# Two tiles of 128x64 in place of four of 128x32 for the projection products of two attention blocks on one core

## The chip, the core and the metric

The kernel runs on one core of a Trainium2 chip. The metric is the device time of one execution in microseconds (us). Beside the times of several runs there is one profiled execution, of which every instruction's start and length is known; its own time and its span (first to last instruction) are given separately.

## What is computed

Two attention blocks, A and B, work on separate inputs of 2048 tokens with 1024 features (32 heads of 32), in bfloat16. Their outputs are put side by side.

```python
# A: plain attention over all 2048 tokens
qkv = x @ wqkv;  p = softmax(q @ k.T * Dh ** -0.5);  a = (p @ v) @ wo
# B: four segments of 512 tokens, one after the other
p = softmax(qs @ ks.T * scale + mask)            # causal within the segment
a_dot = p @ vs
num, den = phi(qs) @ M, phi(qs) @ z + 1e-6       # memory of the segments before
o = g * num / den + (1 - g) * a_dot              # g = sigmoid(beta), per head
M, z = M + phi(ks).T @ vs, z + sum(phi(ks))      # phi(t) = t + 1 if t > 0 else exp(t)
b = o @ wo
```

## The kernel before, in words

**Names of the engines.** PE multiplies matrices, ACT computes exponentials, DVE and POOL do elementwise work, SP issues the transfers. PE holds one operand (the weights, loaded by an instruction of its own) and streams the other past it; the result goes to the memory called `ps`, which has eight banks of 512 float32 columns on 128 rows. The array of 128x128 can be used as several tiles: a tile of 128x32 takes 128 rows of the contraction and gives 32 rows of output, and four of them stand side by side. `tile_position` says where a tile stands.

**The heads in groups.** Four heads make a group of 128 feature columns; A has eight groups, B eight for each segment. For one group the work goes through these stages:

- *Projections.* Queries and keys of a group come out transposed, 128 features by tokens: the weights are a 128x128 block of `W_A` or `W_B`, the streamed operand 512 tokens of `xT_A` or `xT_B`, and eight such steps add up over the 1024 input features (`job_KA`, `job_KB`, through `proj_job`, line 1492). Values come out with tokens on the rows (`job_VA`, line 1697, 256 columns wide; `job_VB`, line 1738). B's memory has two products (`job_mem`, line 1788) and the update of M with its 128-wide steps (`job_M`, line 1810). The output projections run through `job_out` (line 1845), `job_part`, `job_whole` and `job_last` (lines 1921 to 1956). All of these hand a 128x128 block of weights to the helper `mm4` (line 773), which issues it as four tiles of 128x32, each with a matmul of its own on the same streamed operand. In the profile all their instructions stand at line 778. DVE then copies each finished bank out (`evict`, line 1489).
- *Scores* (line 1140). Keys are the weights, queries are streamed; the contraction is one head's 32 features, so four heads run in four tiles of 32x128, 32 rows each.
- *Exponential* (line 1228). ACT takes two banks, 1024 columns, at a time. A part of the exponentials is computed by a polynomial on DVE and POOL (lines 1177, 1186, 1187).
- *Value products and sums* (`round`, line 1286). For each of four heads a tile of 128x32 multiplies 32 value columns with the exponentials (line 1320), and a second set with a matrix of ones gives the row sums (line 1327). They add up in bank 7; afterwards the result is divided by the sums on DVE and POOL.

Two other kinds of product also use tiles of 128x32 and do not go through `mm4`: the guard products of lines 1512 and 1565, which find bounds for the exponential. The values of A's first group (`job_V0`, line 1715) use the whole array, 128x128, at line 1723.

**What sets the order.** Every operation is handed to a planner with an engine, a length in us, a key and the data that it reads and writes (`pe`, line 770, for PE). `schedule` (line 381) goes through a modelled time and puts each engine's operations in a fixed order: scores are urgent and come when ACT will need them, and projections and value products fill PE's time in between. It knows the modes "col" (all 128x32 products and all of the `mm4` ones), "row" (scores) and "full" (line 1723), and adds 0.10 us in the model where the mode changes. Then `rearrange` (line 565) moves single operations by the long written-out list `MOVES`. `emit` turns the dependences into semaphore waits. At run time each engine goes through its own list in order; nothing is reordered between engines but by those waits. Scores have three slots of two banks each (`SLOT_BANKS`), projections one bank (6), so the next projection waits until DVE has emptied it. `halves` (line 1475) cuts a projection step of 512 columns into two of 256, so that the second half of a bank can wait for its copy by itself; where both halves end up next to each other in PE's list, one instruction of 512 columns takes their place.

The helper before:

```python
def mm4(self, e, out, w, x, start, stop):
    for t in range(4):
        r = slice(32 * t, 32 * t + 32)
        ins = e.matmul(out[r], w[:, r], x, start=start, stop=stop, tile_position=(0, 32 * t), skip_group_check=True)
    return ins
```

Of the kernel before, what the change touches and what calls it, by code (L numbers as in the profile page):

```python
# [11 lines left out]
P = 128  # L12
# [6 lines left out]
L = 512  # L19
# [726 lines left out]
class _Kernel:  # L746
# [23 lines left out]
    def pe(self, fn, dur, key, reads=(), writes=(), mode="col"):  # L770
        return self.pg.op("PE", fn, dur, key, reads, writes, mode=mode)

    def mm4(self, e, out, w, x, start, stop):

        ins = None
        for t in range(4):
            r = slice(32 * t, 32 * t + 32)
            ins = e.matmul(out[r], w[:, r], x, start=start, stop=stop, tile_position=(0, 32 * t), skip_group_check=True)  # L778
        return ins

    def dma(self, fn, sem, key, reads=(), writes=(), issue=0.4, lat=3.0, eng="SP", gate=False):
# [710 lines left out]
    def proj_job(self, key, wt, rw, xt, rx, ncol, dst, rdst, behind=None):  # L1492
        b = self.xbank()
        out = self.ps[:, 512 * b:512 * b + ncol]

        self.halves(b, lambda e, i, c, st, en: self.mm4(e, out[:, c], wt[:, i, :], xt(i)[:, c], st, en), 8,
                    lambda i: [rw] + rx(i), dst, out, rdst, key + 1.0, key, behind)

    def square(self, kind, src, rsrc, key):
# [99 lines left out]
    def plan_prologue(self):  # L1599
# [6 lines left out]
        dummy, rd = self.sq["B"][0], self.r_sq["B"][0]  # L1606

        def warm(key, n, dur, behind=None):
            for _ in range(n):
                o = self.pe(lambda e: self.mm4(e, self.ps[:, 512 * 5:512 * 6], dummy[:, 0:P], dummy[:, :], True, True), dur, key,  # L1610
                            [rd], [self.bank[5]])
                if behind:
                    o.order.add(behind)
# [16 lines left out]
        def quarter(key, c, banks):  # L1630
            for i, kq in [(i, kq) for lo in (0, 4) for kq in range(2) for i in range(lo, lo + 4)]:
                    b = banks[kq]
                    o = self.pe(lambda e, i=i, kq=kq, b=b: self.mm4(
                        e, self.ps[:, 512 * b:512 * b + 512], self.WA[0][:, kq, i, :],
                        self.xT[:, i, 512 * c:512 * c + 512], i == 0, i == 7), 0.2165, key,
                        [self.r_WA[0][kq], self.r_xT[i][c]], [self.bank[b]])
                    if c:
                        o.order.add(self.first_ge)
            self.last_quarter = o
            if not c:  # L1640
                warm(key, WARM[1], 0.2165, o)
            sq = []
            for kq in range(2):
                dst = self.KQA[:, 0, kq, 512 * c:512 * c + 512]
                src = self.ps[:, 512 * banks[kq]:512 * banks[kq] + 512]
                bk, rd = self.bank[banks[kq]], self.r_KQA[0][kq][c]
                if c or not kq:
                    self.dve(lambda e, dst=dst, src=src: e.tensor_copy(dst, src), 512, key, [bk], [rd])
                else:
                    self.act(lambda e, dst=dst, src=src: e.activation(dst, src, ACT.Copy), 512, key, [bk], [rd])  # L1650
            for kq in range(2):
                sq += 2 * [self.square("A", self.KQA[:, 0, kq, 512 * c:512 * c + 512], self.r_KQA[0][kq][c], key)]
            if c == 0:
                for x in self.r_KQA[0]:
                    mark(x, "KQ", 0)
                self.colrun = self.guard_cols(key, sq, bank=3)
                self.guard_end(key, [self.colrun], 2, [BIAS_PART[0]], bank=4, urgent=True)
                self.first_ge = self.last_ge
            else:
                self.guard_more(key, sq, 0, *BIAS_PART[:2])  # L1660
                self.early_gc = self.last_gc
# [35 lines left out]
    def job_VA(self, g2, tp, key, bank=None, behind=None):  # L1697
        vs = g2 % 2
        holds(self.r_WAv, "W", g2)
        holds([r[tp // 2] for r in self.r_xT], "x")  # L1700
        mark(self.r_VA[vs][tp], "V", g2)
        b = self.xbank() if bank is None else bank
        dst, src = self.VA[vs][:, 2 * tp:2 * tp + 2, :].rearrange("p a b -> p (a b)"), self.ps[:, 512 * b:512 * b + 512]

        for k in range(2):
            t, c = 2 * tp + k, slice(QC * k, QC * k + QC)
            for i in range(8):
                o = self.pe(lambda e, i=i, t=t, c=c, k=k: self.mm4(e, src[:, c], self.xT[:, i, P * t:P * t + P], self.WAv[:, i, :],
                                                                   i == 0 and k == 0, i == 7), 0.11, key,
                            self.r_WAv + [self.r_xT[i][tp // 2]], [self.at(b)])  # L1710
# [27 lines left out]
    def job_VB(self, s, tt, hh, key):  # L1738
        holds([self.r_WBv], "W", s, hh)
        holds([self.r_xTB], "x", s)  # L1740
        mark([self.r_VB[tt][hh]], "V", s)
        b = self.xbank()
        src, dst = self.ps[:, 512 * b:512 * b + 512], self.VB[:, tt, 512 * hh:512 * hh + 512]

        self.halves(b, lambda e, i, c, st, en: self.mm4(e, src[:, c], self.xTB[:, i, P * tt:P * tt + P], self.WBv[:, i, c], st, en), 8,
                    lambda i: [self.r_WBv, self.r_xTB], dst, src, [self.r_VB[tt][hh]], key + 1.0, key)

    def job_KB(self, s, j, kq, key):
# [39 lines left out]
    def job_mem(self, s, j, key):  # L1788
        holds(self.r_PKQ[j % 2], "P", s, j)
        holds([self.r_Mb[j], self.r_zf[j]], "M", s - 1)  # L1790
        holds(self.r_OTB[j], "out", s - 1)
        mark(self.r_OTB[j], "mem", s)
        PQ = self.PKQ[j % 2][:, 1, :]
        rp = self.r_PKQ[j % 2][1]
        z = j % 2
        self.dve(lambda e: e.tensor_scalar(self.Zb[:, z, :], self.maskbd[:, :], self.zf[:, j:j + 1], None, ALU.mult), P / 2,
                 key - 1.0, [self.r_zf[j], self.r_c], [self.r_Zb[z]])
        b = self.xbank()
        self.pe(lambda e: self.mm4(e, self.ps[:, 512 * b:512 * b + L], self.Zb[:, z, :], PQ, True, True), 0.2165, key,
                [self.r_Zb[z], rp], [self.xr])  # L1800
        T2, r2 = self.recip_rows(self.ps[:, 512 * b:512 * b + L], [self.xr], L, key + 0.3, add=1e-6)
        b2 = self.xbank()
        self.pe(lambda e: self.mm4(e, self.ps[:, 512 * b2:512 * b2 + L], self.Mb[:, j, :], PQ, True, True), 0.2165,
                key, [self.r_Mb[j], rp], [self.xr])
        self.dve(lambda e: e.scalar_tensor_tensor(out=self.OTB[:, j, :], in0=self.ps[:, 512 * b2:512 * b2 + L],
                                                  scalar=self.gc[:, 0, j:j + 1], in1=T2[:, 0:L], op0=ALU.mult,
                                                  op1=ALU.mult), L, key + 0.5, [self.xr] + r2 + [self.r_g],
                 list(self.r_OTB[j]))

    def job_M(self, s, j, key):  # L1810
# [11 lines left out]
        b = self.xbank()  # L1822

        def mm(e, k):
            ins = None
            for t in range(4):
                ins = self.mm4(e, self.ps[:, 512 * b + P * k:512 * b + P * k + P], self.PKt[:, k, P * t:P * t + P],
                               self.VB[:, t, P * (j + k):P * (j + k) + P], t == 0 and k == 0, t == 3)
            return ins
        for k in range(2):  # L1830
# [14 lines left out]
    def job_out(self, kind, row, half, key, lhs, rl, wo, rwo, bank=None, ev="DVE", wcol=None):  # L1845
# [5 lines left out]
        assert ev == "DVE"  # L1851
        wcol = 512 * half if wcol is None else wcol

        self.halves(b, lambda e, j, c, st, en: self.mm4(e, src[:, c], lhs(j), wo(j)[:, wcol:wcol + 512][:, c], st, en), 8,
                    lambda j: rwo(j) + rl(j), ob[:, :], src, [ro], key + 1.0, key)
        col = (0 if kind == "A" else D) + 512 * half
        dst = self.out[0][P * row:P * row + P, col:col + 512]
# [63 lines left out]
    def job_part(self, row, hf, k, key):  # L1921

        b = self.xbank()
        c = row // 2
        src = self.ps[:, 512 * b:512 * b + 512]

        def reads(j):
            holds(self.wo_A(j)[1], "Wo")
            if j < 6:
# [1 line left out]
            return self.wo_A(j)[1] + ([self.r_xT[j][row // 4]] if j < 6 else [self.r_OTx[0][c]])  # L1931
        holds(self.r_KQB[k], "KQ", 3, k)
        mark(self.r_KQB[k], "part", k)
        self.halves(b, lambda e, j, cs, st, en: self.mm4(e, src[:, cs], self.xT[:, j, P * row:P * row + P],
                                                         self.wo_A(j)[0][:, 512 * hf:512 * hf + 512][:, cs], st, en), 7,
                    reads, self.part(k), src, self.r_KQB[k], key + 1.0, key)

# [3 lines left out]
    def job_whole(self, row, hf, k, b, key):  # L1941
# [4 lines left out]
        for j in range(7):  # L1946
            wo, rw = self.wo_A(j)
            holds(rw, "Wo")
            if j < 6:
                holds([self.r_xT[j][row // 4]], "OT")  # L1950
            rx = [self.r_xT[j][row // 4]] if j < 6 else [self.r_OTx[0][row // 2]]
            self.pe(lambda e, j=j, wo=wo: self.mm4(e, src, self.xT[:, j, P * row:P * row + P], wo[:, 512 * hf:512 * hf + 512],
                                                   j == 0, False), 0.2165, key, rw + rx, [self.at(b)])

    def job_last(self, row, hf, k, b, key, ev="DVE"):
# [4 lines left out]
        self.pe(lambda e: self.mm4(e, src, self.xT[:, 7, P * row:P * row + P], wo[:, 512 * hf:512 * hf + 512], ev == "DVE", True),  # L1960
                0.2165, key, rw + [self.r_OTx[1][row // 2]], [self.at(b)])
        ob = self.KQB[:, k, 0, :]
        if ev == "ACT":
# [170 lines left out]
```

## Time and profile before

| | |
|---|---|
| time, median of 3 runs | 1086.79 us (1085.61 to 1088.75) |
| time of the profiled execution | 1085.08 us |
| its span | 1083.3 us |
| matmuls and weight loads on PE | 24,916 each |
| instructions in all | 54,725 |
| mean granted PE clock | 1.00 of full speed |

How to read the rows of the profile. A group's row has the line, the engine, the operation and what it writes and reads; for a matmul or a weight load (LDWEIGHTS, on "PEld") the tile's rows and columns follow (128\*32 is 128 rows by 32 columns), then the shape of the streamed operand, and the count. Behind the bar stand the time in which at least one of them ran, the mean ns of one, and the engine's idle time just before them with what ended it. In a row of the timeline the first number is the start in us from the beginning of the span, the second how long the merged stretch lasted, its modelled end included. Matmuls overlap, so the time that PE needs for one is read from start to start. A row of the table by stage has the stretch, its length, then busy us and count for PE, PEld, DVE, ACT and POOL, the granted PE clock, the mean share of the transfer engines and GB/s. The chain is followed back from the last instruction: at each step to what released it, or to the one before it on its engine.

### The profile page before, as it was taken

The page shows a single profiled execution, that of the slowest core. Times are in us where ns is not written, and L with a number is a line of the kernel's source. Part 1 is how long each engine was busy: PE and PEld are TensorE (multiplying, and loading weights), DVE is VectorE, ACT ScalarE, POOL GpSimd, SP SyncE. Part 2 cuts the span into 40 slices and gives each one's busy share as a digit, 9 for nine tenths or more (in the row PEclk, how much of TensorE's full clock was granted, in tenths as well). Part 3 has the DMA queues.
Part 4 walks back from the last instruction along what each step waited for, and adds up shares of the span by engine and source line. Part 5 has one row for each costly group of instructions (what it writes and reads, how often), then busy time and mean ns, then how long its engine had stood idle before and what let it go on. Part 6 is the DMA issues. An engine that isn't in the chain of part 4 may idle for free.

```text
span 1083.3 us, 54725 instructions
## 1 busy us (share of the span) xinstructions
PE 1029.5 (95%) x24916; PEld 551.4 (51%) x24916; DVE 747.0 (69%) x1639; ACT 1006.5 (93%) x1192; POOL 674.5 (62%) x853
## 2 busy tenths in 40 slices
PE   8999999999999899989999998999999989999997
PEld 4456545556554454456554444465544445445554
DVE  3456667775756988887757898878647788774433
ACT  5999989998999989998999998999999789999997
POOL 1005656676657686977758687777747568866521
PEclk9999999999999999999999999999999999999999
DMA  9032350006212430032321322122121830022101
GB/s 209 8 83 52 80 131 20 11 20 142 53 36 78 114 83 18 6 95 65 87 79 40 76 51 49 26 76 76 33 87 41 247 91 4 32 71 71 42 23 51
DMA packets 171096, 71.96 MB, mean 66 GB/s; under 512 B 134768, under 2 KB 169072, under 8 KB 170864
## 3 DMA queue, kind: packets, MB, share of 16 engines
q1 hardware_dynamic: 168496, 67.66, 25.2%
q8 instruction: 196, 3.21, 1.2%
q10 hardware_dynamic: 2368, 0.79, 0.3%
q14 instruction: 36, 0.29, 0.1%
HBM read 45.23 MB, written 11.67 MB: 53 GB/s over the span
## 4 chain that ended last, share of the span: by engine, by line
PE 51%; ACT 37%; DVE 6%; DMA 2%; issue 2%; POOL 1%; SPq 0%; ACTq 0%; DVEq 0%; POOLq 0%
ACT P L1228 36%; PE ps L778 26%; PE ps L1140 10%; PE ps L1320 7%; PE ps L1327 7%; DMA Wo_B<-in_B_wo_dram 1%; PE ps L1723 1%; DVE Y L1177 1%; DVE T L1345 1%; DVE KQ_B L1490 1%; DMA W_A<-in_A_wqkv_dram 1%; DMA W_B<-in_B_wk_dram 0%; POOL Z L1186 0%; ACT P L1207 0%; PE ps L1512 0%
## 5 line engine op out<-in xcount | busy, mean ns | idle before, releaser
L1228 ACT ACTIVATE P<-ps 128x1024 bf16<-128x1024 f32 (+1 forms) x1176 | 994.8, 988 | 56.8 <-PE ps L1140 24.0
L1186 POOL TENSOR_TENSOR Z<-Y 128x512 f32<-128x512 f32 x280 | 299.5, 1074 | 237.1 <-DVE Y L1177 210.7
L1327 PE MATMUL ps<-P,onesb 128*32 128x256 bf16 (+1 forms) x4400 | 300.2, 270 | 0.1
L1320 PE MATMUL ps<-P,V_A 128*32 128x256 bf16 x3632 | 258.3, 274 | 1.2 <-DVE V_A L1733 0.6
L1177 DVE TENSOR_SCALAR Y<-ps 128x512 f32<-128x512 f32 x232 | 158.9, 685 | 98.9 <-PE ps L1140 94.7
L1140 PE MATMUL ps<-KQ_A 32*128 32x256 bf16 x4096 | 203.7, 272 | 16.1 <-ACT P L1228 8.9
L1187 POOL TENSOR_SCALAR Pc<-Z 128x512 bf16<-128x512 f32 x232 | 149.5, 649 | 23.5 <-PE ps L1320 8.2
L1140 PEld LDWEIGHTS ps<-KQ_A 32*128 32x128 bf16 x4096 | 62.7, 92 | 170.1 <-ACT P L1228 115.8
L1327 PEld LDWEIGHTS ps<-P,onesb 128*32 128x32 bf16 x4400 | 129.1, 96 | 30.9 <-issue 14.6
L778 PE MATMUL ps<-xT_B,W_B 128*32 128x512 bf16 (+1 forms) x2188 | 139.1, 367 | 5.5 <-issue 1.4
L778 PE MATMUL ps<-xT_A,W_A 128*32 128x512 bf16 (+1 forms) x2160 | 137.7, 369 | 1.8 <-DMA W_A<-in_A_wqkv_dram 1.2
L1320 PEld LDWEIGHTS ps<-P,V_A 128*32 128x32 bf16 x3632 | 108.2, 96 | 38.2 <-issue 15.5
L1253 POOL TENSOR_SCALAR_AFFINE_SELECT P<-P 128x768 bf16<-128x768 bf16 (+1 forms) x96 | 75.6, 800 | 71.1 <-ACT P L1228 70.7
L1327 PE MATMUL ps<-Pc,onesb 128*32 128x256 bf16 x464 | 118.6, 273 | 0.0
L1320 PE MATMUL ps<-Pc,V_A 128*32 128x256 bf16 x464 | 118.5, 274 | 0.1
L778 PEld LDWEIGHTS ps<-xT_B,W_B 128*32 128x32 bf16 x2188 | 53.3, 96 | 49.7 <-issue 22.3
L1345 DVE STREAM_TRANSPOSE T<-ps 128x256 f32<-128x256 f32 (+1 forms) x148 | 70.9, 481 | 10.4 <-PE ps L1327 7.5
L778 PEld LDWEIGHTS ps<-xT_A,W_A 128*32 128x32 bf16 x2160 | 51.2, 96 | 45.8 <-issue 12.0
L778 PE MATMUL ps<-Wo_B,OT_B 128*32 128x512 bf16 (+1 forms) x1064 | 71.4, 373 | 2.3 <-DMA Wo_B<-in_B_wo_dram 2.1
L1490 DVE CAST outsb<-ps 128x512 bf16<-128x512 f32 x56 | 38.6, 690 | 50.4 <-PE ps L1320 27.3
L1360 DVE STREAM_TRANSPOSE T<-rc 128x256 f32<-128x256 f32 (+1 forms) x152 | 71.8, 476 | 1.9
L778 PE MATMUL ps<-Wv_B,xT_B 128*32 128x512 bf16 (+1 forms) x1092 | 70.3, 368 | 1.1 <-DVE cols L1519 0.8
(103 smaller groups left out, 1200.1 us busy)
## 6 DMA issues: line engine op xcount, KB each, us to landing
Wv_B<-in_B_wv_dram SPq DMA_DIRECT2D x32, 256.0 KB, 3.8
W_B<-in_B_wk_dram SPq DMA_DIRECT2D x32, 256.0 KB, 3.3
W_B<-in_B_wq_dram SPq DMA_DIRECT2D x32, 256.0 KB, 4.0
Wo_B<-in_B_wo_dram SPq DMA_DIRECT2D x32, 256.0 KB, 3.7
out_dram<-outsb SPq DMA_DIRECT2D x56, 128.0 KB, 1.9
W_A<-in_A_wqkv_dram SPq DMA_DIRECT2D x14, 256.0 KB, 4.5
ot_a_scratch<-OTst SPq DMA_DIRECT2D x50, 64.0 KB, 1.7
xT_A<-ot_a_scratch SPq DMA_DIRECT2D x6, 512.0 KB, 6.7
```

The costliest lines, as they stand in the source:

```text
L778: ins = e.matmul(out[r], w[:, r], x, start=start, stop=stop, tile_position=(0, 32 * t), skip_group_check=True)
L1140: ins = e.matmul(out, kap, qap, start=st, stop=True, tile_position=(32 * h, 0), skip_group_check=True)
L1177: o = self.dve(lambda e: e.tensor_scalar(Y[:, :], src, SCALE, MID, ALU.mult, ALU.add), 512, key - 9.0, [self.bank[bank]], [rY], fixed=0.15)
L1186: self.pool(lambda e: e.tensor_tensor(Z[:, :], Y[:, :], Y[:, :], ALU.mult), 512, key, [rY], [rZ], rate=0.58)
L1187: return self.pool(lambda e: e.tensor_scalar(dst, Z[:, :], C2, REST, ALU.mult, ALU.add), 512, key, [rZ], [rP], rate=TS_RATE)
L1228: a = self.act(guarded if early else lambda e: e.activation(dst, src, ACT.Exp, scale=SCALE), cols, key, rd, wr, fixed=EXP_FIXED)
L1253: self.pool(lambda e: e.affine_select(v, v, pattern=pat, compare_op=ALU.is_ge, fill=0.0, base=0, channel_multiplier=-1), 2 * nd * P, key + ...
L1320: ins = e.matmul(self.ps[32 * h:32 * h + 32, 512 * obk + q0:512 * obk + q0 + nq], v, p, start=first, stop=last, tile_position=(0, 32 * h), ...
L1327: ins = e.matmul(self.ps[32 * h:32 * h + 32, lcol + q0:lcol + q0 + nq], self.onesb[:, 0:32], p, start=False, stop=last, tile_position=(0, ...
L1345: self.dve(lambda e: e.transpose(T2[:, 0:n], src), n, nk, rsrc, [r2], fixed=0.17)
L1360: self.dve(lambda e: e.transpose(T2[:, 0:n].rearrange("p (b r) -> p b r", r=32), bc), n, key, [rr], [r2], fixed=0.17)
L1490: self.dve(lambda e: e.tensor_copy(dst, src), 512, key, [self.at(b)], rdst, fixed=0.155)
```

## The change

The helper now issues two tiles of 64 columns, and has a new name:

```diff
-    def mm4(self, e, out, w, x, start, stop):
+    def mm2(self, e, out, w, x, start, stop):
 
         ins = None
-        for t in range(4):
-            r = slice(32 * t, 32 * t + 32)
-            ins = e.matmul(out[r], w[:, r], x, start=start, stop=stop, tile_position=(0, 32 * t), skip_group_check=True)
+        for t in range(2):
+            r = slice(64 * t, 64 * t + 64)
+            ins = e.matmul(out[r], w[:, r], x, start=start, stop=stop, tile_position=(0, 64 * t), skip_group_check=True)
         return ins
```

Every call of `mm4` becomes one of `mm2`, with the same arguments: in `proj_job`, `warm` and `quarter` (the prologue), `job_VA`, `job_VB`, `job_mem`, `job_M`, `job_out`, `job_part`, `job_whole` and `job_last`. One of them:

```diff
-        self.halves(b, lambda e, i, c, st, en: self.mm4(e, out[:, c], wt[:, i, :], xt(i)[:, c], st, en), 8,
+        self.halves(b, lambda e, i, c, st, en: self.mm2(e, out[:, c], wt[:, i, :], xt(i)[:, c], st, en), 8,
                     lambda i: [rw] + rx(i), dst, out, rdst, key + 1.0, key, behind)
```

The lengths and modes that these calls hand to the planner are untouched, and so are scores, value products, sums and the guard products.

More of the change, by code (lines that the diff above doesn't have):

```diff
@@ L1609, in warm @@
             for _ in range(n):
-                o = self.pe(lambda e: self.mm4(e, self.ps[:, 512 * 5:512 * 6], dummy[:, 0:P], dummy[:, :], True, True), dur, key,
+                o = self.pe(lambda e: self.mm2(e, self.ps[:, 512 * 5:512 * 6], dummy[:, 0:P], dummy[:, :], True, True), dur, key,
                             [rd], [self.bank[5]])
@@ L1632, in quarter @@
                     b = banks[kq]
-                    o = self.pe(lambda e, i=i, kq=kq, b=b: self.mm4(
+                    o = self.pe(lambda e, i=i, kq=kq, b=b: self.mm2(
                         e, self.ps[:, 512 * b:512 * b + 512], self.WA[0][:, kq, i, :],
@@ L1707, in job_VA @@
             for i in range(8):
-                o = self.pe(lambda e, i=i, t=t, c=c, k=k: self.mm4(e, src[:, c], self.xT[:, i, P * t:P * t + P], self.WAv[:, i, :],
+                o = self.pe(lambda e, i=i, t=t, c=c, k=k: self.mm2(e, src[:, c], self.xT[:, i, P * t:P * t + P], self.WAv[:, i, :],
                                                                    i == 0 and k == 0, i == 7), 0.11, key,
@@ L1743, in job_VB @@
         src, dst = self.ps[:, 512 * b:512 * b + 512], self.VB[:, tt, 512 * hh:512 * hh + 512]
-        self.halves(b, lambda e, i, c, st, en: self.mm4(e, src[:, c], self.xTB[:, i, P * tt:P * tt + P], self.WBv[:, i, c], st, en), 8,
+        self.halves(b, lambda e, i, c, st, en: self.mm2(e, src[:, c], self.xTB[:, i, P * tt:P * tt + P], self.WBv[:, i, c], st, en), 8,
                     lambda i: [self.r_WBv, self.r_xTB], dst, src, [self.r_VB[tt][hh]], key + 1.0, key)
@@ L1798, in job_mem @@
         b = self.xbank()
-        self.pe(lambda e: self.mm4(e, self.ps[:, 512 * b:512 * b + L], self.Zb[:, z, :], PQ, True, True), 0.2165, key,
+        self.pe(lambda e: self.mm2(e, self.ps[:, 512 * b:512 * b + L], self.Zb[:, z, :], PQ, True, True), 0.2165, key,
                 [self.r_Zb[z], rp], [self.xr])
@@ L1802, in job_mem @@
         b2 = self.xbank()
-        self.pe(lambda e: self.mm4(e, self.ps[:, 512 * b2:512 * b2 + L], self.Mb[:, j, :], PQ, True, True), 0.2165,
+        self.pe(lambda e: self.mm2(e, self.ps[:, 512 * b2:512 * b2 + L], self.Mb[:, j, :], PQ, True, True), 0.2165,
                 key, [self.r_Mb[j], rp], [self.xr])
@@ L1826, in mm @@
             for t in range(4):
-                ins = self.mm4(e, self.ps[:, 512 * b + P * k:512 * b + P * k + P], self.PKt[:, k, P * t:P * t + P],
+                ins = self.mm2(e, self.ps[:, 512 * b + P * k:512 * b + P * k + P], self.PKt[:, k, P * t:P * t + P],
                                self.VB[:, t, P * (j + k):P * (j + k) + P], t == 0 and k == 0, t == 3)
@@ L1852, in job_out @@
         wcol = 512 * half if wcol is None else wcol
-        self.halves(b, lambda e, j, c, st, en: self.mm4(e, src[:, c], lhs(j), wo(j)[:, wcol:wcol + 512][:, c], st, en), 8,
+        self.halves(b, lambda e, j, c, st, en: self.mm2(e, src[:, c], lhs(j), wo(j)[:, wcol:wcol + 512][:, c], st, en), 8,
                     lambda j: rwo(j) + rl(j), ob[:, :], src, [ro], key + 1.0, key)
@@ L1933, in job_part @@
         mark(self.r_KQB[k], "part", k)
-        self.halves(b, lambda e, j, cs, st, en: self.mm4(e, src[:, cs], self.xT[:, j, P * row:P * row + P],
+        self.halves(b, lambda e, j, cs, st, en: self.mm2(e, src[:, cs], self.xT[:, j, P * row:P * row + P],
                                                          self.wo_A(j)[0][:, 512 * hf:512 * hf + 512][:, cs], st, en), 7,
@@ L1951, in job_whole @@
             rx = [self.r_xT[j][row // 4]] if j < 6 else [self.r_OTx[0][row // 2]]
-            self.pe(lambda e, j=j, wo=wo: self.mm4(e, src, self.xT[:, j, P * row:P * row + P], wo[:, 512 * hf:512 * hf + 512],
+            self.pe(lambda e, j=j, wo=wo: self.mm2(e, src, self.xT[:, j, P * row:P * row + P], wo[:, 512 * hf:512 * hf + 512],
                                                    j == 0, False), 0.2165, key, rw + rx, [self.at(b)])
@@ L1959, in job_last @@
         src = self.ps[:, 512 * b:512 * b + 512]
-        self.pe(lambda e: self.mm4(e, src, self.xT[:, 7, P * row:P * row + P], wo[:, 512 * hf:512 * hf + 512], ev == "DVE", True),
+        self.pe(lambda e: self.mm2(e, src, self.xT[:, 7, P * row:P * row + P], wo[:, 512 * hf:512 * hf + 512], ev == "DVE", True),
                 0.2165, key, rw + [self.r_OTx[1][row // 2]], [self.at(b)])
```

## The prediction

> **What bounds the kernel now.** I read the page's busy shares first, then the shares of the chain that ended last.
>
> ```profile
> span 1083.3 us, 54725 instructions
> ...
> PE 1029.5 (95%) x24916; PEld 551.4 (51%) x24916; DVE 747.0 (69%) x1639; ACT 1006.5 (93%) x1192; POOL 674.5 (62%) x853
> ...
> PE 51%; ACT 37%; DVE 6%; DMA 2%; issue 2%; POOL 1%; SPq 0%; ACTq 0%; DVEq 0%; POOLq 0%
> ```
>
> Two engines are nearly full, and the chain changes hands between them. PE issues scores, ACT exponentiates them, and PE spends the time between two score blocks on value products, sums and projections. Everything else carries about a tenth of the chain. A busy share cannot say which of the two limits a given stretch, because matmul ends are modelled and overlap. So I took the chain piece by piece: it gives stretches that belong to PE alone and stretches that belong to ACT alone. Two of the latter, from the chain in order of time:
>
> ```profile
> 220.41 24.09 ACT P L1228 x28
> ```
>
> ```profile
> 992.50 49.20 ACT P L1228 x59
> ```
>
> And this is what the engines did in a PE stretch (540 to 570, in which the chain is PE but for 0.1%) and in the second ACT stretch, from the table by stage:
>
> ```profile
> 540.00:570.00 30.00, 29.97 (x708) 15.05 (x700) 15.05 (x32) 29.44 (x37) 17.35 (x22) 1.00 0.30 82
> 992.50:1041.50 49.00, 48.73 (x1168) 25.33 (x1156) 22.27 (x43) 49.00 (x59) 23.93 (x31) 1.00 0.19 60
> ```
>
> The first two sums are PE matmuls and weight loads, the fourth is ACT. In the PE stretch PE never rests; in the ACT stretch ACT never rests, yet PE has only some tenths of a microsecond to spare in 49 us. The clock granted is 1.00 in both. So whatever lengthens PE's work shows up in the first kind of stretch in full, and soon in the second.
>
> **The change part by part.** The order on every engine stays: the planner is handed the same durations and the same mode name for these products, and the number of semaphore updates is the same. What changes is inside each call of the helper.
>
> *Fewer instructions.* The rows of line 778 run from the largest to the smallest of eleven groups (the middle one, of A's values, is used further down):
>
> ```profile
> L778 PE MATMUL ps<-xT_B,W_B 128*32 128x512 bf16 (+1 forms) x2188 | 139.1, 367 | 5.5 <-issue 1.4 <-DVE cols L1519 1.2 <-DMA W_B<-in_B_wk_dram 1.2
> ...
> L778 PE MATMUL ps<-Wv_A,xT_A 128*32 128x256 bf16 x1536 | 53.4, 274 | 2.8 <-issue 2.3 <-DVE cols L1573 0.4
> ...
> L778 PE MATMUL ps<-sqB 128*32 128x512 bf16 x92 | 6.8, 458 | 1.3 <-DVE sqB L1614 1.3
> ```
>
> Together they are 9,700 matmuls and as many weight loads, in 2,425 steps of four. Half of each go, 9,700 of PE's 49,832 records. That saves no streaming: the four tiles of a step run side by side, and so will two. The next fence shows it: a projection step of 512 columns (303.57) holds PE for 0.22 us until the next start, and 256-wide steps come every 0.11 us; these are 512 and 256 columns at 2.4 per ns. What the 9,700 records can save is a few ns where a run ends.
>
> *Steps of one kind in a row.* The same fence shows sums, a projection step and value products in the present kernel, all in tiles of 128x32:
>
> ```profile
> 303.47 0.28 PE L1327 MATMUL ps<-P,onesb 128*32 128x256 bf16 x3
> 303.57 0.39 PE L778 MATMUL ps<-Wo_B,OT_B 128*32 128x512 bf16 x4
> 303.79 0.27 PE L1320 MATMUL ps<-Pc,V_A 128*32 128x256 bf16 x1
> ...
> 303.90 0.27 PE L1327 MATMUL ps<-Pc,onesb 128*32 128x256 bf16 x1
> ...
> 304.01 0.28 PE L1320 MATMUL ps<-P,V_A 128*32 128x256 bf16 x4
> ```
>
> From sum to projection 0.10 us, from projection to value product 0.22 us: going over costs nothing today. After the change the middle step has another tile shape than its neighbours.
>
> *What a new tile shape costs.* Two places of this trace show it: the score blocks, in tiles of 32x128, and line 1723, a value projection of A's first group in the undivided 128x128 array.
>
> ```profile
> 300.77 0.29 PE L1320 MATMUL ps<-P,V_A 128*32 128x256 bf16 x4
> 300.99 0.40 PE L1140 MATMUL ps<-KQ_A 32*128 32x256 bf16 x8
> 301.32 0.29 PE L1327 MATMUL ps<-P,onesb 128*32 128x256 bf16 x4
> ```
>
> ```profile
> 56.57 0.28 PE L1327 MATMUL ps<-P,onesb 128*32 128x256 bf16 x4
> 56.79 0.29 PE L1723 MATMUL ps<-Wv_A,xT_A 128*128 128x128 bf16 x2
> ```
>
> ```profile
> 89.21 0.22 PE L1723 MATMUL ps<-Wv_A,xT_A 128*128 128x128 bf16 x1
> 89.36 0.40 PE L1140 MATMUL ps<-KQ_A 32*128 32x256 bf16 x8
> 89.69 0.34 PE L1723 MATMUL ps<-Wv_A,xT_A 128*128 128x128 bf16 x3
> 89.96 0.29 PE L1320 MATMUL ps<-P,V_A 128*32 128x256 bf16 x4
> ```
>
> Value product to scores: 0.22 us for 0.107 us of columns, so 0.11 lost. Scores back: 0.33 for 2 x 0.107, so 0.11 with the second step's own extra. 128x32 to 128x128 (56.57): 0.22 for 0.107, again 0.11. Back (89.69): 0.27 for 3 x 0.053, 0.11. In the last two only the width of the tile changes, as it will here. No row shows 32 to 64 columns. Its price is bounded by the 128x32 to 128x32 rows (0.00) and by these (0.11); below nothing it cannot be, since a step in line already loses nothing. I take 0.10, since all four kinds of crossing that change the shape agree, whichever dimension changes.
>
> The Trainium skill says the same in general ("TensorEngine Tiling (Array Packing)", Key Properties): a change of tiling mode, not merely of tile, drains the array. It lists 128x64 and 128x32 as separate modes; by it the crossing is paid, and the rows above agree in kind.
>
> *How many crossings.* Going through PE's list in order of time, I counted neighbours of which one is a line 778 step and the other another 128x32 step. First and last that lie between value products or sums and a projection:
>
> ```profile
> 25.71 0.28 PE L1320 MATMUL ps<-P,V_A 128*32 128x256 bf16 x4
> 25.82 0.39 PE L778 MATMUL ps<-xT_A,W_A 128*32 128x512 bf16 x4
> ```
>
> ```profile
> 1075.53 0.28 PE L1327 MATMUL ps<-P,onesb 128*32 128x256 bf16 x4
> 1075.64 0.39 PE L778 MATMUL ps<-V_A,xT_A 128*32 128x512 bf16 x4
> ```
>
> There are 389 in and 387 out, and 6 beside the guard products of lines 1512 and 1565: 782 in all, 78 us of PE time. Crossings between projections and scores are paid already and stay. By the chain, 421 of the 782 lie in PE's pieces, 301 in ACT's and 60 in the rest.
>
> *The sum.* (a) PE's pieces: 421 x 0.10 = 42 us, less some 4 us where PE waits at that very place anyhow (over all 782 such waits cover 12 us). (b) ACT's pieces: 301 x 0.10 = 30 us. How much PE idles there is bounded by the waits view, first by the load rows of scores, then by PE's own:
>
> ```profile
> PEld ps L1140 <- ACT P L1228: 133.8, 376, 1.4
> ```
>
> ```profile
> PE ps L1140 <- ACT P L1228: 10.5, 30, 1.0
> ```
>
> 376 waits of 0.356 us, of which 0.21 is the last step's columns and the crossing, leave 376 x 0.146 = 55 us at most; 10.5 is the least. Between them, PE's starts one by one leave 28 us of idle time beyond columns and crossings in ACT's pieces. It lies unevenly: in the 49.2 us stretch above stand 37 crossings (3.7 us) against 0.6 us of idle, in the 24.1 us one 16 (1.6 us) against 1.3. Stretch by stretch, 11 us do not fit; the ends are 2 us, if all idle could be used anywhere, and 30 us, if none. I take 11. (c) The other 60: 6 us, of which half counts, for those pieces wait on transfers and on DVE, which itself often waits for PE: 3 us. (d) Fewer instructions: 128x128 to scores (89.21) takes 0.15 for 0.053, about 0.10, against 0.11 from four tiles; 0.01 at 312 crossings from projections to scores, half on PE's chain: -1 us. Sum 42 - 4 + 11 + 3 - 1 = **+51 us**. The profiled execution took 1085.1 us (span 1083.3), so 1136; the median of the three runs, 1086.8, stands 1.7 us above it, which gives **1137 us**.
>
> What is late next:
>
> ```profile
> L1228 ACT ACTIVATE P<-ps 128x1024 bf16<-128x1024 f32 (+1 forms) x1176 | 994.8, 988 | 56.8 <-PE ps L1140 24.0
> ```
>
> the next score block stands behind the projection run in PE's queue, so its start slips, ACT's exponential with it, and then the value products that read it. ACT will show more than these 56.8 us idle, with PE as releaser.
>
> **The rivals.**
>
> *No drain between 32 and 64 columns* (the side that is not slower). Both shapes use all 128 rows; if the array separates columns by mask alone, a crossing stays at 0.00 and only (d) is left: 1085 to 1087. It decides by the price of a crossing: below about 0.01 us (782 x 0.01 x 0.65 = 5 us, less 1) the change cannot be told from none, and gains over 3 us have no source. Against it: 128x32 to 128x128 also keeps the rows and pays 0.11.
>
> *Loads of 64 columns that do not hide.* Load rows do not grow with width now:
>
> ```profile
> L778 PEld LDWEIGHTS ps<-xT_A,W_A 128*32 128x32 bf16 x2160 | 51.2, 96 | 45.8 <-issue 12.0 <-DMA W_A<-in_A_wqkv_dram 1.7 <-DVE KQ_A L1490 1.7
> ...
> L1723 PEld LDWEIGHTS ps<-Wv_A,xT_A 128*128 128x128 bf16 x256 | 14.4, 98 | 4.0 <-issue 3.0 <-DVE cols L1573 0.5 <-DVE sqA L1503 0.2
> ```
>
> If two loads ran one after the other, each for its whole record, a step would need 0.19 us: hidden under 512 columns (0.213), not under 256 (0.107). The 256-wide steps (1,536 of V's for A and 856 in six smaller groups, by four: 598) would lose 0.085 each, 51 us, and the 96 of 128 columns 0.14 each, 13 us; with 0.65 (51 of 78) of that on the path, 42 us on top: 1179. Against it: line 1723 loads 128 columns for each 128-wide matmul and holds its pace (89.69).
>
> The Trainium skill ("TensorE: Matmul & The Clock Gate", LDWEIGHTS) puts a load at its columns over 1.2 per ns, an estimate of 53 ns for 64 columns: two in a row would just equal 256 columns and only the 96 narrow steps would lose, about 5 us of PE time. No run here shows a 64-column load.
>
> *All spare time is used* (slower, but less). If ACT's lead of up to three score slots lets PE use every idle moment in ACT's stretches, (b) is 2 and (a) loses its covered part fully: 42 - 12 + 2 = 32, less 1 to 7 for pieces (c) and (d) that fall away: 1112 to 1119.
>
> *No spare time is used*: every crossing lengthens the span, 78 - 1: 1164.
>
> **How the numbers follow.** The paid crossing, with its span from all to no idle used, has 0.85: 1112 to 1163. No drain has 0.09: 0.06 within 0.3% of before (about 3 us, what a measurement of this kernel can tell from no change), 0.03 faster. Loads that show have 0.06, slower. The range leaves both out. So faster 0.03, same 0.06, slower 0.91.
>
> **What the profile would show.** Line 778 would read 128*64 with half the counts (1,094 for B's keys and queries), streaming pitch 0.216 us unchanged. From a sum to a projection the start-to-start time would be 0.21 instead of 0.11; from a single projection step to a value product 0.32 instead of 0.22. PE's share of the chain would rise above 51%, ACT's fall, and the idle time before ACT's line 1228 would grow. I am wrong if those two times stay, or if they rise and the span does not; and the 64-column loads are to blame if 256-wide projection steps come slower than 0.11 us.

## The result, and the profile after

| | before | after |
|---|---|---|
| time, median | 1086.2 us (1085.55 to 1088.75, 4 runs) | 1143.72 us (1143.52 to 1144.11, 4 runs) |
| ratio, 95% interval | | 1.0528, 1.0506 to 1.0549 |
| profiled execution, its span | 1085.08, 1083.3 us | 1143.52, 1141.7 us |
| matmuls and weight loads on PE | 24,916 each | 20,016 each |

The change makes the kernel 5.3% slower. The forecast was 1137 us, with a range from 1112 to 1163.

The page of the changed kernel, in the lines that answer to those of before: the busy shares, the chain, and ACT's main group.

```profile
span 1141.7 us, 44925 instructions
...
PE 1104.5 (97%) x20016; PEld 533.2 (47%) x20016; DVE 746.2 (65%) x1639; ACT 1027.7 (90%) x1192; POOL 674.1 (59%) x853
...
PE 86%; DVE 8%; ACT 4%; DMA 1%; issue 1%; ACTq 0%; DVEq 0%
...
L1228 ACT ACTIVATE P<-ps 128x1024 bf16<-128x1024 f32 (+1 forms) x1176 | 1016.0, 947 | 93.6 <-PE ps L1140 49.6
```

PE had 51% of the chain and has 86%; ACT had 37% and has 4%. PE issues a fifth fewer instructions and is busy longer. ACT idles 93.6 us ahead of line 1228 where it idled 56.8, mostly until scores arrive.

The place that the prediction showed at 303.47, the same instructions in the timeline of the changed kernel:

```profile
320.55 0.29 PE L1327 MATMUL ps<-P,onesb 128*32 128x256 bf16 x3
320.77 0.41 PE L778 MATMUL ps<-Wo_B,OT_B 128*64 128x512 bf16 x2
321.10 0.28 PE L1320 MATMUL ps<-Pc,V_A 128*32 128x256 bf16 x1
...
321.22 0.27 PE L1327 MATMUL ps<-Pc,onesb 128*32 128x256 bf16 x1
...
321.33 0.28 PE L1320 MATMUL ps<-P,V_A 128*32 128x256 bf16 x4
```

From sum to projection it is now 0.22 us and was 0.10; from the projection to the value product 0.33 and was 0.22. The next step (321.22) is 0.12 behind, the one after that 0.11, as always.

A stretch with several steps in each run shows a second thing:

```profile
570.79 0.84 PE L778 MATMUL ps<-Wv_B,xT_B 128*64 128x512 bf16 x6
571.56 0.29 PE L1320 MATMUL ps<-P,V_A 128*32 128x256 bf16 x4
571.78 0.62 PE L778 MATMUL ps<-Wv_B,xT_B 128*64 128x512 bf16 x4
572.34 0.40 PE L1140 MATMUL ps<-KQ_A 32*128 32x256 bf16 x8
```

The run that starts at 571.78 has two steps, and the scores start 0.56 us behind it: 0.43 are columns, 0.10 the crossing, and 0.03 are left. Taken over all runs, start to start, the first step behind a crossing lasts longer than its columns by 0.027 us with 64-column tiles, by 0.013 with tiles of 32 columns, by 0.013 with the whole array and by 0.013 with the 32x128 tiles of scores; later steps by 0.0025.

**Where the 58 us came from.** Every start-to-start time of PE's steps can be split into its columns (at 2.4 per ns), what such a neighbour always costs (the lower quartile of its kind) and the rest, which is waiting. Summed over PE's list, to about 2 us, in us (a kind is a tile shape, whether the step is the first of its shape, and the next tile shape):

| | columns | crossings and starts | waiting | span |
|---|---|---|---|---|
| before | 843 | 151 | 83 | 1083.3 |
| after | 843 | 242 | 52 | 1141.7 |

(The few us before the first and behind the last step make up the rest.) So PE got 91 us of work that streams nothing, and 31 us of it went where PE had been waiting. The split depends a little on the kinds: told apart by their columns too, they give 246 and 46 for the changed kernel and leave the row of before as it is. The waits view agrees. These are the load rows of scores that wait for ACT in the changed kernel, then PE's own row:

```profile
PEld ps L1140 <- ACT P L1228: 68.5, 190, 1.4
```

```profile
PE ps L1140 <- ACT P L1228: 4.2, 13, 0.9
```

They were 133.8 us in 376 waits and 10.5 in 30.

The two stretches that the prediction looked at, found again by their exponentials, in the table by stage of the changed kernel:

```profile
567.60:599.60 32.00, 32.00 (x548) 14.03 (x548) 15.01 (x30) 29.79 (x37) 16.77 (x22) 1.00 0.23 66
1044.20:1097.40 53.20, 53.09 (x949) 24.42 (x941) 22.53 (x43) 51.19 (x59) 23.82 (x30) 1.00 0.17 54
```

The 35 exponentials that lie whole in 540 to 570 took 29.5 us from the start of the first to the end of the last; they take 32.0. The stretch that was ACT's alone took 49.2 and takes 53.2 for the same 59 exponentials; ACT now rests 2 us in it, and the chain there is PE's.

### The profile page after: what moved, and what is told of

The parts are those of the page before. It is cut to its first block, busy times and chain, and to the rows that moved or that the text cites. A ratio compares the mean times of both kernels' runs of the same rounds, so it can differ in the third digit from the quotient of the medians.

```text
span 1141.7 us, 44925 instructions
## 1 busy us (share of the span) xinstructions
PE 1104.5 (97%) x20016; PEld 533.2 (47%) x20016; DVE 746.2 (65%) x1639; ACT 1027.7 (90%) x1192; POOL 674.1 (59%) x853
## 4 chain that ended last, share of the span: by engine, by line
PE 86%; DVE 8%; ACT 4%; DMA 1%; issue 1%; ACTq 0%; DVEq 0%
PE ps L778 43%; PE ps L1140 15%; PE ps L1320 14%; PE ps L1327 12%; ACT P L1228 4%; PE ps L1723 1%; DVE T L1345 1%; DVE Y L1177 1%; DVE KQ_B L1490 1%; DVE OT_B L1805 1%; PE ps L1512 1%; DVE KQ_A L1490 1%; DMA W_A<-in_A_wqkv_dram 1%; DMA W_B<-in_B_wk_dram 1%; ACT P L1207 0%
## 5 line engine op out<-in xcount | busy, mean ns | idle before, releaser
L1228 ACT ACTIVATE P<-ps 128x1024 bf16<-128x1024 f32 (+1 forms) x1176 | 1016.0, 947 | 93.6 <-PE ps L1140 49.6
L778 PE MATMUL ps<-xT_B,W_B 128*64 128x512 bf16 (+1 forms) x1094 | 141.3, 372 | 3.2 <-DVE cols L1519 1.2
L778 PE MATMUL ps<-xT_A,W_A 128*64 128x512 bf16 (+1 forms) x1080 | 140.9, 375 | 1.6 <-DMA W_A<-in_A_wqkv_dram 1.2
L778 PEld LDWEIGHTS ps<-xT_B,W_B 128*64 128x64 bf16 x1094 | 52.7, 108 | 56.6 <-issue 30.2
L778 PEld LDWEIGHTS ps<-xT_A,W_A 128*64 128x64 bf16 x1080 | 50.5, 109 | 55.7 <-issue 20.4
L1490 DVE CAST outsb<-ps 128x512 bf16<-128x512 f32 x56 | 38.6, 690 | 57.3 <-PE ps L778 53.2
L778 PE MATMUL ps<-Wo_B,OT_B 128*64 128x512 bf16 (+1 forms) x532 | 73.2, 379 | 0.2 <-DVE outsb L1490 0.2
L778 PE MATMUL ps<-Wv_B,xT_B 128*64 128x512 bf16 (+1 forms) x546 | 71.9, 373 | 0.9 <-DVE cols L1519 0.8
```

Of the source, the lines that this page charges most:

```text
L1228: a = self.act(guarded if early else lambda e: e.activation(dst, src, ACT.Exp, scale=SCALE), cols, key, rd, wr, fixed=EXP_FIXED)
L1490: self.dve(lambda e: e.tensor_copy(dst, src), 512, key, [self.at(b)], rdst, fixed=0.155)
```

## The experiments

Each ran beside the kernel before on one chip; ratios are to that. Two theories stood against each other. **Crossing**: what costs is the change of tile shape between projections and value products, as plain PE time. **Tile**: steps of 64 columns are slow in themselves. To choose tiles run by run, several kernels mark, in the finished order of PE's list, the runs of projection steps by what stands beside them, and ask for the mark when a step is issued.

**No crossing, all tiles of 64 columns.** The value products follow the projections, and the sums in the same way:

```diff
-                v = vt[:, c0 + 32 * h:c0 + 32 * h + 32]
+                v = vt[:, c0 + 32 * (h - h % 2):c0 + 32 * (h - h % 2) + 64]
...
-                for h, v, p, q0, nq, first, last in tiles:
-                    ins = e.matmul(self.ps[32 * h:32 * h + 32, 512 * obk + q0:512 * obk + q0 + nq], v, p, start=first, stop=last,
+                for h, v, p, q0, nq, first, last in tiles[::2]:
+                    ins = e.matmul(self.ps[32 * h:32 * h + 64, 512 * obk + q0:512 * obk + q0 + nq], v, p, start=first, stop=last,
```

> The changed kernel, with value products and sums also issued as two tiles of 128x64 (tiles of heads 0 and 2 with 64 columns each), so that no crossing between projections and value products is left. It leaves out the products of heads 1 and 3 with their own exponentials: their output rows hold the values of heads 1 and 3 weighted by the exponentials of heads 0 and 2. Theory (the crossing between tile widths costs PE about 0.1 us, and the first step behind it a little more): the 782 added crossings are gone, what is left is the longer first step behind 563 score blocks (0.014 each, 8 us of PE) less some ns at their ends; back to 1086 to 1091 us. Rival (tiles of 64 columns are slow in themselves, by their loads or their streaming): at least the 1144 us of the changed kernel, more with more of them.

1080.68 us, ratio 0.9943 (0.9922 to 0.9964). The whole loss is gone though there are more 64-column steps than ever; the tile theory falls. The same kind of neighbours in its timeline:

```profile
545.64 0.30 PE L1320 MATMUL ps<-P,V_A 128*64 128x256 bf16 x2
545.78 0.28 PE L1327 MATMUL ps<-P,onesb 128*64 128x256 bf16 x2
545.88 0.28 PE L1320 MATMUL ps<-P,V_A 128*64 128x256 bf16 x2
545.99 0.81 PE L778 MATMUL ps<-Wv_B,xT_B 128*64 128x512 bf16 x6
```

Value product to projection is 0.11 us again; only the first step behind the scores (545.64) has its 0.14. It even came out below the expected 1086 to 1091, faster than before: by the split above its list has 13 us more of crossings and starts than before, and 16 us less of waiting. The last experiment tells a part of why.

**The whole array for projections.** One matmul of 128x128 per step:

```diff
-        for t in range(2):
-            r = slice(64 * t, 64 * t + 64)
-            ins = e.matmul(out[r], w[:, r], x, start=start, stop=stop, tile_position=(0, 64 * t), skip_group_check=True)
+        for t in range(1):
+            r = slice(128 * t, 128 * t + 128)
+            ins = e.matmul(out[r], w[:, r], x, start=start, stop=stop, skip_group_check=True)
```

> The changed kernel with each projection step as one matmul of the whole 128x128 array. Theory (any change of tile shape costs): all 782 crossings stay, at 0.108 in and 0.096 out as line 1723 shows them; the first step behind a crossing loses 0.010 as at line 1723 and not 0.024 as with 64 columns, and the way into scores is 0.010 shorter; PE carries about 82 us more than before where the changed kernel carries 93; 1136 to 1141 us. Rival (64 columns are the slow thing): about the 1086 us of before. Second rival (the first step's loss grows with the width of the load): 0.053 behind each of some 700 crossings, 1150 us and more.

1134.92 us, ratio 1.0443 (1.0420 to 1.0465), 1 us below the range; 9 us faster than the changed kernel, 48 slower than before. So the loss is not a matter of 64 columns: the whole array, another shape than the neighbours' too, brings most of it. The second rival, 1150 us and more, falls as well. The 9 us have the size of the shorter first step (0.013 for 0.027 in some 700 runs, about 10 us of PE) and way into scores; they were not taken apart. This trace has 17,331 matmuls beside 17,566 weight loads, so some 235 matmul records are missing, and its time is used and not its sums.

**64 columns where no crossing arises, and the reverse.** Runs are marked by their neighbours; the tile width follows the mark:

```diff
+        c = 64 if self.pg.cur.wd else 32
+        for t in range(P // c):
+            r = slice(c * t, c * t + c)
+            ins = e.matmul(out[r], w[:, r], x, start=start, stop=stop, tile_position=(0, c * t), skip_group_check=True)
...
+        col = (a == "col") + (b == "col")
...
+        if not col:
...
+            for n in r:
+                q[n].wd = "w"
```

Here `a` and `b` are the modes of what stands ahead of the run `r` and behind it. The reverse has `if col:` in place of `if not col:`, the half has `if not col or seen % 2:`, where `seen` counts the runs beside other 128x32 work.

> The kernel before, with 64-column tiles only in those runs of projection steps that stand between two score blocks: 92 runs, 546 of the 2,458 steps, and not one added crossing. Theory: 1086 to 1088 us, since only the first step of 92 runs is longer by 0.014 and the way into scores shorter by 0.007. Rival (64-column steps are slow in themselves): 22% of the steps, so 22% of the loss, 1099 us.

1087.51 us, ratio 1.0005 (0.9993 to 1.0016): 22% of the steps in 64-column tiles change nothing that can be measured, and the rival's 1099 us falls.

> The reverse of the run with 64 columns between score blocks alone: 64-column tiles only in the 611 runs beside other 128x32 work, 1,912 steps and all 782 added crossings; the 92 runs between score blocks stay at 32 columns. Theory: as the changed kernel, 1141 to 1145 us. Rival (the loss goes with the steps): 78% of it, 1131 us.

1143.48 us, ratio 1.0516 (1.0479 to 1.0553): the runs beside other 128x32 work carry the whole loss, and not the rival's 78% of it.

**Half of the crossings.**

> 64-column tiles in the 92 runs between two score blocks and in every second one of the 611 runs that stand beside other 128x32 work: about 394 of the 782 added crossings, 1,543 of the 2,458 steps. Theory (each added crossing is about 0.117 us of PE time with its first step, 91 us in the changed kernel, of which 31 went into PE's waits): 46 us on PE; at least half and at most three quarters of the 31 us of waits are used up for it, so 21 to 30 us more than before, 1108 to 1117 us. Rival (the loss goes with the steps of 64 columns): 63% of it, 1122 us.

1111.2 us, ratio 1.0219 (1.0183 to 1.0255): as the theory has it, and below the rival's 1122. Its split of PE's time is 843 columns, 196 crossings and starts, 65 waiting: 45 us of the 91, and 18.5 of the 31 us of waits are already used up. The first half of the crossings cost 25 us of span, the second half 33.

**The same PE time without a crossing.** At each place where the change crosses, the kernel before gets one more step in its old shape, first within the projection (behind a run's first step, or behind its last):

```diff
+    return [(out, w, x, start, stop and not k)] + [(out[:, 0:n], self.zer[:, :], x[:, 0:n], False, stop and i == k - 1) for i in range(k)]
```

> The kernel before, all projections in four tiles of 32 columns, with one more step of up to 256 columns (0.107 us, weights of zeros, so it adds nothing to the result) at each place where the change crosses between projections and other 128x32 work, some 775 of them. No tile shape changes. Theory (a crossing is nothing but PE time): 83 us more on PE, of which 0.63 reaches the span as in the changed kernel (58 of 93 us); 1134 to 1142 us. Rival (the loss comes from something else that the shape change brings, such as loads that can't run ahead or hand-overs that slip): plain PE time finds PE's idle moments, at most half of the loss, 1115 us or less.

1163.43 us, ratio 1.0707 (1.0679 to 1.0734): far more than forecast, and not the rival either. The padding came to 84 us of columns (some 810 steps, since the four-part steps of B's memory update get four each), and the span grew by 79.6; waiting fell from 83 to 78 only. So my share of 0.63 does not hold for just any PE time.

Then with the padding ahead of the bordering value product or sum:

```diff
-                ins = None
+                ins = pads(self, e, tiles, 512 * obk)
```

> The kernel before, with the padding steps of the earlier padding run (a step of zeros of up to 256 columns, no new tile shape) moved out of the projections: each stands ahead of the value product or sum that borders the run, about 770 of them. Theory (the earlier padding cost more than the crossings, 77 us for 84, because it lengthened the chain from a projection's first step to the copy that frees its only bank, which a crossing does not): 1140 to 1150 us. Rival (padding costs more because it can't run while PE waits, as an emptying array can, wherever it stands): 1158 to 1165 us.

1148.82 us, ratio 1.0568 (1.0530 to 1.0605). 80 us of columns, 62.9 us of span, waiting 65. That is the theory's range and not the rival's. Where the time stands matters: inside a projection it costs 0.95 of itself, outside 0.79, as a crossing 0.64. A part of these distances is not the place, though: the padded kernels have more instructions and with them more of the idle moments that the last experiment is about (8.5 and 6.6 us, where before has 3.6), the changed kernel has none. If such moments reach the span in full, the shares without them are about 0.89, 0.75 and 0.68, an estimate from these figures. In ACT's row, first with the padding inside, then outside:

```profile
L1228 ACT ACTIVATE P<-ps 128x1024 bf16<-128x1024 f32 (+1 forms) x1176 | 1019.1, 943 | 111.8 <-PE ps L1140 63.7 <-PE ps L1327 29.2 <-PE ps L778 3.3
```

```profile
L1228 ACT ACTIVATE P<-ps 128x1024 bf16<-128x1024 f32 (+1 forms) x1176 | 1015.4, 946 | 98.8 <-PE ps L1140 53.4 <-PE ps L1327 28.3 <-DVE T L1360 3.2
```

ACT idles 111.8 and 98.8 us where the changed kernel has 93.6. That a step inside the projection delays the copy which frees its only bank is my reason for the difference; it fits, but only the place is shown. That a crossing is a little cheaper still would agree with its 0.10 us running while PE waits anyhow (such waits covered 12 us in the prediction's count), which padding, issued behind the wait, can't do. No run shows this, and it was not taken apart further.

**The whole array where no crossing arises.** As the run with 64 columns between score blocks, with `c = 128`:

> The kernel before, with one matmul of the whole array per step in the 92 runs between two score blocks alone, so that no crossing is added; 3,276 of PE's 49,832 records go. Theory (crossings cost, and PE now and then stands without instructions in the middle of a step, 3.6 us in the profile of before and none in the changed kernel, which has fewer of them): the way from a run into scores is 0.010 shorter, 1 us in all, and some of the 3.6 us go: 1083 to 1086 us beside 1086.6. Rival (the idle moments in mid-step have nothing to do with the number of instructions): 1085.5 to 1087.

1085.75 us beside 1087.21, ratio 0.9981 (0.9965 to 0.9997): faster than both kernels, by no more than 0.35%. The time lies in the theory's range and in the rival's too, so this run does not decide between them: it has fewer instructions and a shorter way into scores, and the interval does not tell the two reasons apart.

**More instructions, same columns.** The waits view of before has four places where PE stops within a run and no wait is seen. One of them, from the timeline:

```profile
858.30 0.61 PE L778 MATMUL ps<-xT_B,W_B 128*32 128x512 bf16 x7
860.26 1.05 PE L778 MATMUL ps<-xT_B,W_B 128*32 128x512 bf16 x16 [1.35 <-issue]
```

Seven matmuls of two steps are issued, and the eighth comes 1.35 us after PE fell idle. The waits view sums them up for the kernel before:

```profile
PE ps L778 <- issue: 3.6, 4, 1.4
```

In the changed kernel and in the one with all tiles of 64 columns there is no such row. To see whether the number of instructions makes them, two halves of a step are never joined:

```diff
-                    pair = e == "PE" and o.twin is not None and at[e] + 1 < len(q) and q[at[e] + 1] is o.twin
+                    pair = False and o.twin is not None and at[e] + 1 < len(q) and q[at[e] + 1] is o.twin
```

> The kernel before, with the two halves of a projection step always issued as two steps of 256 columns, never as one of 512: some 12,000 records more on PE, the same columns, no new tile shape, no other order. The steps themselves cost about 0.0025 us each for some 1,550 more, 4 us. Theory (PE stands without instructions in mid-step when there are too many of them; 3.6 us in the profile of before with 49,832 records, none in the changed kernel with 40,032): more than twice the idle moments in mid-step, 8 us or more, and 1093 to 1100 us. Rival (those moments have nothing to do with the number of instructions): about 3.6 us of them again, 1089 to 1092 us.

1104.61 us beside 1090.26, ratio 1.0113 (1.0067 to 1.0159), even above the range; the kernel before took 3 to 4 us more on this chip than on the two others, which makes up a part of that. Its waits:

```profile
PE ps L778 <- issue: 6.0, 7, 2.0
PE ps L1320 <- issue: 3.7, 5, 2.1
PE ps L1140 <- issue: 3.6, 4, 1.8
...
PE ps L1327 <- issue: 1.9, 3, 1.1
```

15.2 us in 19 places with 62,880 matmul and load records on PE, 3.6 with 49,832, none with 40,032: these moments come with the number of instructions. The other complete traces agree: none with 30,304 (all tiles of 64 columns) and 42,216 (the reverse), 0.5 with 43,684 (the half), 3.1 with 47,648, 6.6 and 8.5 in the two padded kernels with 55,992 and 56,336. So the change also won up to 3.6 us, which lie in the 58 as a gain. The kernel with all tiles of 64 columns won them too, against a lead of 4.3 us in the profiled executions; the rest was not taken apart.

What PE waits for can be read from the transfers. The pages of before and of this run count a queue that brings instructions:

```profile
q8 instruction: 196, 3.21, 1.2%
```

```profile
q8 instruction: 247, 4.05, 1.6%
```

Each of these packets has 16,384 bytes, and in both runs there is one for some 254 matmul and load records. In the complete traces PE stops 51 times for 0.1 us or more without a wait that is seen, and each time it goes on 1.2 to 1.6 us behind the landing of such a packet. A time picked at random lies so behind one in 7 to 10 of 100 cases. So PE stands there until its next block of instructions has come. What makes a block come late was not tested.

The distance to before is larger than the added stops. The profiled executions are 21.3 us apart: 11.6 are stops and 3.7 the longer list of steps. The rest is mostly the clock, which was granted at half for three windows of 3.41 us. Most of each lies in one of these rows (the 0.50 is the clock):

```profile
258.60:261.80 3.20, 3.20 (x60) 1.74 (x60) 0.69 (x1) 1.94 (x2) 0.00 (x0) 0.50 0.02 5
859.30:862.60 3.30, 3.30 (x62) 1.85 (x56) 0.48 (x1) 1.94 (x2) 0.68 (x1) 0.50 0.03 8
876.40:879.60 3.20, 3.18 (x63) 2.43 (x65) 0.16 (x2) 0.60 (x1) 0.00 (x0) 0.50 1.21 293
```

Half the clock for 10.2 us is 5.1 us lost, an estimate. Each window begins within 1.1 us of the end of a stop of 1.8 to 2.1 us; a fourth stop of that length (1.93 us, at 491.58) has none behind it, and no other trace here has such a window in its midst.

## Why the prediction was right, and by how much its terms were off

- *The bound.* PE and ACT both nearly full, and PE's added time mostly on the path: right. The chain and ACT's idle time moved as said.
- *No saving from fewer instructions but (d).* Wrong by up to 3.6 us: the moments in mid-step stood in the profile of before, under "issue", and I did not price them. The eleven groups also add up to 9,800 matmuls in 2,450 steps, not 9,700 in 2,425; the sum does not use that number.
- *The price of a crossing, 0.10.* Into 64 columns the list has 0.103 over a step in line, out of them 0.097: right. The rows taken from 128x32 to the whole array foretold it, and the rule of the Trainium skill ("TensorEngine Tiling (Array Packing)", Key Properties) that the prediction quoted, a drain at each change of tiling mode, agrees with these 0.10 us for 64 against 32 columns too. What I left out is the first step behind a crossing: 0.024 more with 64 columns (some 700 runs, where 310 had begun behind scores before with 0.010 more) and 0.010 more for value products that now follow a crossing. With these, 782 crossings are 91 us by the split above, 0.117 each, and not 77; added up from the parts they are 94. The rows of before showed a small part of it: value product to scores and back, I read 0.11 for the crossing and noted the second step's own extra of 0.010, and then dropped that extra from the price. That 64 columns have 0.024, no row of before could show.
- *The rival of loads that do not hide.* Wrong as put: steps of 256 columns keep their pace behind the first one (0.109 us from start to start). The first step's extra, once for each run, may be a load that does not hide; no run separates that from the crossing. It is 27 ns for 64 columns and 13 for 32, which is their number at 2.4 per ns, but also 13 for the whole array's 128. The load formula of the Trainium skill that I set beside it ("TensorE: Matmul & The Clock Gate", LDWEIGHTS), an estimate of 53 ns for 64 columns, would by my reading have slowed the steps of 128 columns; in the changed kernel they follow each other at 0.055 to 0.056 us, their columns and 0.002, so two such loads in a row do not show.
- *How much reaches the span.* Of 77 us I let 26 vanish; of 91, 31 did. The share was right, its parts less so, and that they balanced is luck: the 25 long ACT stretches grew by 20 to 23 us, depending on where their ends are taken, and not 11 (the 49.2 us one by 4.0, the 24.1 us one by 1.3), the rest by 35 to 38 and not 40. Idle moments within one ACT stretch were less usable than a sum over the stretch says.
- *The other rivals.* No drain: refuted by the timeline and by the run with all tiles of 64 columns. All or no idle time used: the measured case lies between, as the forecast did. (The upper end of the first should read 1118, 32 less 1 and not 32.)

The sum forecast was +51 us; measured +58.4 in the profiled executions. The term that was mis-sized is the crossing, 14 us of PE time short, with 5 us more absorbed than forecast.

## What to carry to other kernels

Where PE changes between tile shapes, count the changes in its order of issue before anything else: here each cost 0.10 us, and 0.117 with the longer first steps behind it, a little more than a whole step of 256 columns. Choosing a tile shape for one kind of product was free here only where its neighbours had the same shape or where a crossing was paid anyhow. Whether added PE time reaches the span depends on where it stands: 84 us of padding within the projections cost 80, 80 us ahead of the value products cost 63, and 91 us of crossings cost 58. Count the instructions too: the padding cost some of that by its instructions alone, and the change won up to 3.6 us by having fewer.

## What the runs showed of the hardware that was not expected

- The first step behind a change of shape lasts longer by 0.027 us with 64-column tiles, 0.013 with 32-column tiles and 0.013 with the whole 128x128 array. Later steps have 0.0025.
- PE stands still, up to 2.1 us at a time and with no wait in the trace, when it is given many short instructions: 0, 3.6, 8.5 and 15.2 us in all with 40,032, 49,832, 56,336 and 62,880 matmul and load records. All 51 such stops end 1.2 to 1.6 us behind the landing of a packet of 16,384 bytes of the queue that brings instructions, some 254 records each.
- In the run whose halves are never joined, three of its four stops of 1.8 to 2.1 us have a window of 3.41 us at half the granted clock beside their end.
